# Fixed transfer order and GpSimd-issued shuffles in the first batch of a spectral mixture-of-experts kernel

## The chip, the cores and the metric

The kernel runs on one core of a Trainium2 chip. The metric is the device time of one execution in microseconds (us), lower is better. The engines are called by the profile's names: PE (TensorE matmul), PEld (its weight loads), DVE (VectorE), ACT (ScalarE), POOL (GpSimd) and SP (SyncE, which only issues transfers). ACT, POOL and SP each have a queue from which they can issue DMA transfers; the lines of the profile call these issues SPq, ACTq and POOL.

## The reference

```python
def _attn_ref(x, filt_r, filt_i):            # x [8, 3072, 256] float32
    X = np.fft.rfft(x, axis=1)
    return np.fft.irfft(X * (filt_r + 1j * filt_i)[None], n=3072, axis=1)

def _moe_ref(x, w_a, w_b, w_out):            # float64 weights, hidden size 1536
    return (x @ w_a) * (x @ w_b) @ w_out

def _moe2_ref(x, w_gate, w_output_gate, w1, w2):   # 8 experts, hidden size 1024
    logits = x @ w_gate
    e_idx = argmax(logits); p = softmax(logits)
    eom = sigmoid(x @ w_output_gate)
    out[mask_e] = p[mask_e, e] * eom[mask_e, e] * (relu(x[mask_e] @ w1[e]) @ w2[e])   # each expert e
```

The 24,576 tokens pass a spectral filter along the sequence, a gated feed-forward block, and then one of eight experts each.

## The kernel before, in words

The transform of length 3072 is split as 96 times 32. Stage 1 multiplies along the first factor, a shuffle of rows follows, stage 2 multiplies along the second factor, applies the filter and goes back over it, and stage 3 goes back over the first factor. After that the tokens go in 64 tiles of 384 through the first feed-forward block (`moe1`), whose 12 chunks of the hidden size (index f) each need a chunk of weights that has been turned from float64 into two float32 halves. Batches 1 to 7 are transformed beside the tiles of earlier batches. Batch 0 has nothing to run beside, and `conv_first` does it: this is the stage that the change touches, and the first tile of `moe1` waits for its end.

`conv_first` works as follows.

- Stage 1 has 16 steps u. Each loads a 192 KB tile of x (`load_x`, L310) on SP, multiplies it by f1f (L338) and copies the result on ACT (L339) into `stay`, a buffer on chip that later holds weight chunks 4 to 11. The x tiles rotate through 6 buffers, five of them filled ahead.
- Stage 2 has 12 units m. A unit reads its shuffled rows a2 (`load_a2`): two transfers of 128 KB from `stay` to an x-type buffer, each from 4 partitions to 128 partitions (L329). All 24 are issued from SP, four units ahead. All of stage 1 must be done before the first, since each reads all columns.
- A unit also needs `load_c`: the filter rows fg (256 KB, L315) and the matrices cr (384 KB, L322), on SP, three units ahead; unit 0 also reads fr (256 KB, L319).
- Then follow 4 matmuls into psx (L351), two shuffles of the filter on DVE (L364), two products px and qx on DVE (L367, L368), 8 matmuls into psb (L376), a copy on ACT (L379) and a 256 KB store to b_dr on ACT's queue (L380).
- After the last unit `s3_load` reads bt from b_dr on SP (L392), stage 3 runs on PE (L399), and the first tile of `moe1` begins (its first matmul is the one into pa at L113).

Beside it runs `weight_steps`. A chunk is loaded by three transfers of 256 KB on SP (L663 twice, L667) into one of four buffers. Step `first` works on ACT and DVE (L680 to L682), `second` on DVE, ACT and POOL (L687 to L694; the POOL product is L694), `third` on PE, ACT, POOL and DVE (L700 to L713; the POOL subtraction is L118, wab<-ws), `fourth` forms the gate columns (L720, L721). The load of chunk f + 4 has to wait for `second` of chunk f, whose buffer it takes. The loop in the program part says how many of these steps stand among the 40 steps of `conv_first`, from step n_first on; with N_EARLY = 3 there are 18 of them. The rest stand in the first tile of `moe1`, four per chunk.

The order in which each engine's queue takes its instructions is not the program's order: a scheduler in the build simulates the kernel and orders each queue by its own times. Only from tile 60 on is SP's order that of the program (`manual_schedule`).

Of the kernel before, what the change touches and what calls it, by code (L numbers as in the profile page):

```python
# [9 lines left out]
F32 = mybir.dt.float32  # L10
# [9 lines left out]
B, S, D = 8, 3072, 256  # L20
NTOK = B * S
NE, DFF, DFF2 = 8, 1536, 1024
# sequence index n = 32 * n1 + n2, frequency k = k1 + 96 * k2
N1, N2 = 96, 32
# [7 lines left out]
# routed tokens: expert e owns rows [e * CAP, (e + 1) * CAP) of the bucket buffer  # L32
# [3 lines left out]
def _phases():  # L36
    """Token counts per weight load, largest first, and how many such groups are sure to exist;
    the last kind has as many as could be needed."""
    out, used = [], 0
    for t, seen in ((2048, SNAP * MT), (1024, SNAP * MT), (512, NTOK)):  # L40
        n = -(-(seen - used - NE * (t - 1)) // t)
        out.append((t, n))
        used += t * n
    t = 256
    out.append((t, (NTOK - used + NE * (t - 1)) // t))
    return out
# [4 lines left out]
CAP = NTOK + T_B  # L51
DUMMY = NE * CAP
BIG_ID = 1 << 20
# high words, read as float32, of the float64 numbers 2**-126 and just under 2**128
F64_MIN, F64_MAX = (float(v) for v in np.array([897 << 20, (1151 << 20) - 1], np.int32).view(np.float32))
# batches that go through the convolution together, and the tiles in which they do
ROUNDS = (((1,), 1, 6), ((2, 3), 6, 16), ((4, 5), 16, 32), ((6, 7), 32, 48))
# chunks of the first block's weights that are ready before its first tile
N_EARLY = 3
# chunks whose place is not lent to the first convolution  # L60
F_STAY = FC - N2 * D // 1024
# groups of the last kind at its end that are run only if some token needs them
# [4 lines left out]
def spectral_moe_kernel(ctx: ExitStack, tc: tile.TileContext, a: dict, out: bass.AP):  # L67
# [30 lines left out]
    # by chunk of the hidden size: high and low halves of w_a and w_b  # L98
# [10 lines left out]
    def split3(ps, terms, start, stop):  # L109
        """Products of operands given as (high, low) pairs, all but low * low."""  # L110
        n = len(terms)
        for i, ((lh, ll), (rh, rl)) in enumerate(terms):
            nc.tensor.matmul(ps, lhsT=lh, rhs=rh, start=start and i == 0, stop=False)  # L113
            nc.tensor.matmul(ps, lhsT=lh, rhs=rl, start=False, stop=False)  # L114
            nc.tensor.matmul(ps, lhsT=ll, rhs=rh, start=False, stop=stop and i == n - 1)  # L115
# [5 lines left out]
    a_dr, b_dr = {}, {}  # L121

    def conv_steps(bs):
        """Emission steps of some batches' convolution, up to its inverse over n2; each step
        says whether it is of the tensor engine or of the others."""
        vp = pool["v"]
        nb = len(bs)
        # a unit of stage 2 is one group of rows of two batches, or two groups of one
# [77 lines left out]
        # stage 1  # L206
# [25 lines left out]
        # stage 2 and its inverse  # L232
# [61 lines left out]
    def conv_first():  # L294
        """The convolution of batch 0, before there is other work: the tensor engine has time
        for float32 products, which need no split operands, and for a product more instead of
        an exchange of rows. What stage 1 makes stays on chip, where weights come later."""
# [9 lines left out]
        def load_x(u):  # L307
            if u < half:
                xin[u] = vp.tile([N1, 2, D], F32, tag="xin", name="xin", bufs=6)
                nc.sync.dma_start(xin[u], xv[:, 2 * u : 2 * u + 2, :])  # L310

        def load_c(u):
            if u < n_u:
                fg[u] = mp.tile([128, 2, D], F32, tag=("xth", "xtl")[u % 2], name="fg")
                nc.sync.dma_start(fg[u], a["fri"][2 * u : 2 * u + 2].rearrange("t p d -> p t d"))  # L315
                if u == 0:
                    # its first row pairs two real frequencies: the real parts come row by row
                    fr0 = vp.tile([128, 2, D], F32, tag="fr", name="fr0")
                    nc.sync.dma_start(fr0, a["frfi"][0:2, :, 0].rearrange("t p d -> p t d"))  # L319
                    fg[0] = fg[0], fr0  # L320
                cr[u] = vp.tile([128, 3, 2, 128], F32, tag="cr", name="cr", bufs=6)
                nc.sync.dma_start(cr[u], a["c_first"][u])  # L322

        def load_a2(u):
            if u < n_u:
                a2[u] = vp.tile([128, 2, D], F32, tag="xin", name="a2", bufs=6)
                for j in range(2):
                    k = 4 * (2 * u + j)
                    nc.sync.dma_start(a2[u][:, j, :], stay[k : k + 4].rearrange("k (n d) -> k n d", d=D))  # L329

        for u in range(5):
            load_x(u)
        for u in range(half):
            load_x(u + 5)
            if u in (4, 6, 8):
                load_c(u // 2 - 2)
            p = ps_cv("ps1", 2 * D, N1)
            nc.tensor.matmul(p, lhsT=f1f, rhs=xin.pop(u).rearrange("p n d -> p (n d)"), start=True, stop=True)  # L338
            nc.scalar.copy(stay[:, 2 * D * u : 2 * D * (u + 1)], p)  # L339
            yield  # L340
        for u in range(4):
            load_a2(u)
        xx = {}
        for m in range(n_u + 1):
            load_c(m + 3)
            load_a2(m + 4)
# [87 lines left out]
    def gate_1(i):  # L434
        z = ztile[i]
        lg, og = z[:, :, D : D + NE], z[:, :, D + NE : D + 2 * NE]
        m = small("gm", [128, 3, 1])
        nc.vector.tensor_reduce(out=m, in_=lg, axis=AX.X, op=ALU.max)
        d = small("gd", [128, 3, NE])
        nc.vector.tensor_tensor(out=d, in0=lg, in1=bc(m), op=ALU.subtract)  # L440
        e = small("ge", [128, 3, NE])
        nc.scalar.activation(e, d, AF.Exp)
        # the first of equal maxima: the largest of 8 - index
        r = small("gr", [128, 3, NE])
        nc.vector.scalar_tensor_tensor(
            out=r, in0=d, scalar=0.0, in1=rev.unsqueeze(1).to_broadcast([128, 3, NE]), op0=ALU.is_ge, op1=ALU.mult
        )
        nc.vector.tensor_reduce(out=m, in_=r, axis=AX.X, op=ALU.max)
        oh = small("goh", [128, 3, NE])
        nc.vector.tensor_tensor(out=oh, in0=r, in1=bc(m), op=ALU.is_equal)  # L450
        ob = small("gob", [128, 3, NE], BF16)
        nc.vector.tensor_copy(ob, oh)
        osel = small("gos", [128, 3, NE])
        nc.vector.tensor_tensor(out=osel, in0=oh, in1=og, op=ALU.mult)
        o = small("go", [128, 3, 1])
        nc.vector.tensor_reduce(out=o, in_=osel, axis=AX.X, op=ALU.add)
        eo = small("geo", [128, 3, 1])
        nc.scalar.activation(eo, o, AF.Exp, scale=-1.0)
        gate[i] = (e, oh, ob, eo)
# [19 lines left out]
    def gate_2(i):  # L479
# [18 lines left out]
        # scale = 1 / (sum + 1e-9) / (1 + exp(-o))  # L498
# [63 lines left out]
    def plan(k, start, end):  # L562
        """Expert and first row of each group of kind k among the rows [start, end) of each
        expert; groups past the last one get the dummy rows. Returns the rows left."""
# [57 lines left out]
    def plan_rest(c):  # L622
# [3 lines left out]
        # rows past the last of each expert: no token, scale 0  # L626
# [7 lines left out]
    def load_consts():  # L634
        nc.sync.dma_start(sgn, a["c_sgn"])
        nc.sync.dma_start(f1f, a["c_f1f"])
        nc.sync.dma_start(w3, a["c_w3"])

    def load_consts_2():
        nc.gpsimd.dma_start(f1, a["c_f1"])  # L640
# [7 lines left out]
    def weight_steps():  # L648
        """Float64 weights, one 128-wide chunk of the hidden size at a time: float32 values from
        their bits, exact halves of these, and the gate columns."""  # L650
# [21 lines left out]
        def first(f):  # L672
# [6 lines left out]
            # magnitudes in float32's normal range; the exponent's offset 1023 becomes 127  # L679
# [16 lines left out]
        def third(f):  # L696
# [14 lines left out]
            # gate columns: w_out @ [w_gate | w_output_gate]  # L711
# [24 lines left out]
    # groups that share one load of weights, and their tiles of up to 512 tokens  # L736
# [98 lines left out]
    def l2(n, c):  # L835
# [6 lines left out]
        for j in range(nj):  # L842
            p = psy[n][j // 2][:, 256 * (j % 2) : 256 * (j % 2 + 1)]
            bl = slice(128 * j, 128 * (j + 1))
            # both halves of a bank accumulate; the first product issued there clears it
# [30 lines left out]
    def moe2_slot(n, c, pre=True):  # L876
        """Slot c of tile n of the routed block, with what its successors need."""
# [20 lines left out]

    load_consts()
# [9 lines left out]
    n_first = 8  # L909
    early = 4 * N_EARLY + 7  # L910
    done = 0
    for n, _ in enumerate(conv_first()):
        if n == 4:
            load_consts_2()
# [5 lines left out]
    s3_load(0)  # L920
    for k in range(2):
        s3_mm(0, k)
# [104 lines left out]
    # the last groups, which few distributions of the tokens need  # L1027
# [33 lines left out]
def _constants():  # L1061
# [46 lines left out]
    # of batch 0: also the matrix for the product with the filter's imaginary part, which  # L1108
    # enters the partner's row
# [52 lines left out]
```

## Time and profile before

| What | Value |
|---|---|
| Median of 3 runs | 4187.19 us (4184.61 to 4190.07) |
| Span of the profiled execution, first to last instruction | 4183.0 us |
| PE busy | 4064.7 us, 97% of the span |
| DVE, ACT, POOL busy | 2059.5 (49%), 1819.5 (43%), 724.5 us (17%) |
| DMA | 346.73 MB, mean 83 GB/s |

The profile gives the profiled execution by its span alone; the median of the timed runs is 4.2 us above that span, and that difference stands for what lies before the first and after the last instruction. A line of the timeline gives the start, the duration, the engine, the line of the kernel, the operation, out<-in and how many were merged (x4); in brackets stand the idle time of the engine ahead of it and what ended it. A line of the window view gives for each engine the busy time and the number of instructions, then the granted clock of TensorE (1.00 is 2.4 GHz, 0.50 is 1.2 GHz), the mean busy share of the 16 DMA engines and the bytes moved.

### The profile page before, as it was taken

What the parts mean: (1) busy time and instruction counts of PE and PEld (TensorE: products, weight loads), DVE (VectorE), ACT (ScalarE), POOL (GpSimd) and SP (SyncE); (2) the same over time, 40 slices, a digit from 0 to 9 for tenths busy, and PEclk for the clock granted to TensorE, in tenths of its full rate; (3) what the DMA queues carried; (4) which work ended last, traced back from release to release, by engine and by line L of the source; (5) the groups of instructions that cost most, each with busy time, mean ns of one, the idle gap of its engine ahead of it and who ended that gap; (6) DMA issues with size and microseconds to landing.
All of it is one profiled execution on the core that took longest, in us unless ns stands there. A gap on an engine that the chain in (4) does not pass through costs nothing. (4 is left out here: it accounts for less than half of the span.)

```text
span 4183.0 us, 68755 instructions
## 1 busy us (share of the span) xinstructions
PE 4064.7 (97%) x26500; PEld 3895.0 (93%) x26500; DVE 2059.5 (49%) x4496; ACT 1819.5 (43%) x3832; POOL 724.5 (17%) x672
## 2 busy tenths in 40 slices
PE   5699999999999999999999999999999999999998
PEld 2599999999999999999999999999999999999998
DVE  3556456644465554445554444445433333444575
ACT  2455455544444443444443333333333343444565
POOL 1313013310022210012221000000111111111211
PEclk7699999999999999999999999999999999999999
DMA  5444233312222211222221000001221222234364
GB/s 161 136 129 131 73 99 106 97 55 79 76 69 72 76 58 53 73 69 74 71 66 39 19 22 20 20 20 37 74 69 65 75 95 95 84 128 143 124 218 144
DMA packets 214625, 346.73 MB, mean 83 GB/s; under 512 B 22956, under 2 KB 134285, under 8 KB 214290
## 3 DMA queue, kind: packets, MB, share of 16 engines
q1 hardware_dynamic: 156658, 242.99, 19.2%
q10 hardware_dynamic: 38656, 47.20, 3.6%
q0 software_dynamic: 18976, 52.07, 3.4%
q8 instruction: 210, 3.44, 0.3%
q14 instruction: 125, 1.02, 0.1%
HBM read 237.50 MB, written 102.38 MB: 81 GB/s over the span
## 5 line engine op out<-in xcount | busy, mean ns | idle before, releaser
L540 ACT CAST gh<-g 128x384 fp32r<-128x384 f32 x768 | 394.1, 513 | 833.6 <-DVE g L539 818.8
L539 DVE TENSOR_TENSOR g<-asb,pb 128x384 f32<-128x384 f32 x768 | 424.3, 552 | 632.9 <-PE pb L115 617.1
L115 PE MATMUL po<-wo_h,gl 128*128 128x272 f32 x2304 | 664.6, 288 | 0.0
L114 PE MATMUL po<-wo_l,gh 128*128 128x272 f32 x2304 | 663.4, 288 | 0.0
L118 DVE TENSOR_TENSOR gl<-g,gh 128x384 fp32r<-128x384 f32 x768 | 464.3, 605 | 403.1 <-ACT gh L540 402.3
L113 PE MATMUL po<-wo_h,gh 128*128 128x272 f32 x2304 | 662.5, 288 | 0.0
L532 ACT COPY asb<-pa 128x384 f32<-128x384 f32 x768 | 368.6, 480 | 438.7 <-PE pa L115 437.1
L830 DVE SCALAR_TENSOR_TENSOR hl<-ph,hh 128x512 fp32r<-128x512 f32 (+1 forms) x464 | 284.1, 612 | 528.4 <-ACT hh L829 525.4
L113 PE MATMUL pa<-xth,wab 128*128 128x384 f32 x1536 | 537.2, 350 | 4.0 <-ACT asb L532 3.9
L113 PE MATMUL pb<-xth,wab 128*128 128x384 f32 x1536 | 518.0, 337 | 2.5 <-DVE g L539 2.4
L115 PE MATMUL pa<-xth,wab 128*128 128x384 f32 x1536 | 520.1, 339 | 0.0
L114 PE MATMUL pa<-xtl,wab 128*128 128x384 f32 x1536 | 518.9, 338 | 0.0
L114 PE MATMUL pb<-xtl,wab 128*128 128x384 f32 x1536 | 516.8, 336 | 0.0
L115 PE MATMUL pb<-xth,wab 128*128 128x384 f32 x1536 | 515.6, 336 | 0.0
L829 ACT ACTIVATE hh<-ph 128x512 fp32r<-128x512 f32 (+1 forms) x464 | 250.7, 540 | 547.0 <-PE ph L115 545.9
L503 POOL DMA_INDIRECT zbuf<-z,gpi x192 | 201.1, 1048 | 1636.6 <-ACT asb L532 1054.7
L113 PEld LDWEIGHTS po<-wo_h,gh 128*128 128x128 f32 x2304 | 434.3, 188 | 0.0
L115 PEld LDWEIGHTS po<-wo_h,gl 128*128 128x128 f32 x2304 | 433.3, 188 | 0.2 <-DVE gl L118 0.2
L114 PEld LDWEIGHTS po<-wo_l,gh 128*128 128x128 f32 x2304 | 432.7, 188 | 0.0
L864 POOL DMA_INDIRECT out<-y,z x198 | 204.4, 1032 | 954.2 <-ACT y L863 560.9
L113 PEld LDWEIGHTS pa<-xth,wab 128*128 128x128 f32 x1536 | 289.3, 188 | 16.5 <-ACT asb L532 5.2
L114 PEld LDWEIGHTS pa<-xtl,wab 128*128 128x128 f32 x1536 | 289.7, 189 | 9.5 <-DVE xtl L118 0.3
(178 smaller groups left out, 8078.2 us busy)
## 6 DMA issues: line engine op xcount, KB each, us to landing
raw<-in_moe_w SPq DMA_DIRECT2D x156, 512.0 KB
xin<-in_x SPq DMA_DIRECT2D x128, 192.0 KB
b_dr<-bsb ACTq DMA_DIRECT2D x96, 256.0 KB
bt<-b_dr SPq DMA_DIRECT2D x64, 384.0 KB
z<-zbuf SPq DMA_DIRECT2D x41, 544.0 KB
a_dr<-asb ACTq DMA_DIRECT2D x112, 192.0 KB
a<-a_dr SPq DMA_DIRECT2D x84, 256.0 KB
fg<-in_frfi SPq DMA_DIRECT2D x72, 256.0 KB
```

What stands on the lines that cost most here:

```text
L113: nc.tensor.matmul(ps, lhsT=lh, rhs=rh, start=start and i == 0, stop=False)
L114: nc.tensor.matmul(ps, lhsT=lh, rhs=rl, start=False, stop=False)
L115: nc.tensor.matmul(ps, lhsT=ll, rhs=rh, start=False, stop=stop and i == n - 1)
L118: eng.tensor_tensor(out=o, in0=x, in1=h.bitcast(F32), op=ALU.subtract)
L503: nc.gpsimd.indirect_dma_start(out=zbuf, out_offset=bass.IndirectOffsetOnAxis(ap=posi[:, j : j + 1], axis=0), in_=z[:, j, :], in_offset=No ...
L532: nc.scalar.copy(asb, pa)
L539: nc.vector.tensor_tensor(out=g, in0=asb, in1=pb, op=ALU.mult)
L540: nc.scalar.copy(gh, g)
L829: nc.scalar.activation(hh[:, :t], p[:, :t], AF.Relu)
L830: nc.vector.scalar_tensor_tensor(out=hl[:, :t], in0=p[:, :t], scalar=0.0, in1=hh[:, :t].bitcast(F32), op0=ALU.max, op1=ALU.subtract)
L864: nc.gpsimd.indirect_dma_start(out=out, out_offset=bass.IndirectOffsetOnAxis(ap=z[:, j, D + 1 : D + 2].bitcast(I32), axis=0), in_=y, in_of ...
```

## The change

The change concerns only what happens up to the end of batch 0's transform, with one constant for the weights. SP's transfers of that part keep the program's order (`manual_schedule` around it), and the program's order is rearranged: of the constants only f1f is loaded ahead of x, and x has 8 tiles ahead. The 24 shuffle transfers a2 are issued from GpSimd's queue instead of SP's, six units ahead. `load_c` of units 0 to 3 stands in stage 1 (at u = 3, 5, 7, 9), later ones behind a2 in their unit. N_EARLY goes from 3 to 4 and n_first from 8 to 6, so that 22 weight steps stand among the 40. Comments were taken out as well.

```diff
-N_EARLY = 3
+N_EARLY = 4
+AHEAD = 8
...
         def load_x(u):
             if u < half:
-                xin[u] = vp.tile([N1, 2, D], F32, tag="xin", name="xin", bufs=6)
+                xin[u] = vp.tile([N1, 2, D], F32, tag="xin", name="xin", bufs=AHEAD)
                 nc.sync.dma_start(xin[u], xv[:, 2 * u : 2 * u + 2, :])
...
         def load_a2(u):
             if u < n_u:
-                a2[u] = vp.tile([128, 2, D], F32, tag="xin", name="a2", bufs=6)
+                a2[u] = vp.tile([128, 2, D], F32, tag="xin", name="a2", bufs=AHEAD)
                 for j in range(2):
                     k = 4 * (2 * u + j)
-                    nc.sync.dma_start(a2[u][:, j, :], stay[k : k + 4].rearrange("k (n d) -> k n d", d=D))
-
-        for u in range(5):
+                    nc.gpsimd.dma_start(a2[u][:, j, :], stay[k : k + 4].rearrange("k (n d) -> k n d", d=D))
+
+        for u in range(AHEAD):
             load_x(u)
         for u in range(half):
-            load_x(u + 5)
-            if u in (4, 6, 8):
-                load_c(u // 2 - 2)
+            load_x(u + AHEAD)
+            if u in (3, 5, 7, 9):
+                load_c((u - 3) // 2)
...
-        for u in range(4):
+        for u in range(AHEAD - 2):
             load_a2(u)
         xx = {}
         for m in range(n_u + 1):
-            load_c(m + 3)
-            load_a2(m + 4)
+            load_a2(m + AHEAD - 2)
+            if m:
+                load_c(m + 3)
...
     def load_consts():
+        nc.sync.dma_start(f1f, a["c_f1f"])
+
+    def load_consts_2():
         nc.sync.dma_start(sgn, a["c_sgn"])
-        nc.sync.dma_start(f1f, a["c_f1f"])
         nc.sync.dma_start(w3, a["c_w3"])
-
-    def load_consts_2():
         nc.gpsimd.dma_start(f1, a["c_f1"])
...
+    stack_sp = ExitStack()
+    stack_sp.enter_context(tc.manual_schedule(engines={mybir.EngineType.SP}))
     load_consts()
...
-    n_first = 8
+    n_first = 6
     early = 4 * N_EARLY + 7
...
-        if n == 4:
+        if n == 5:
             load_consts_2()
...
     s3_load(0)
+    stack_sp.close()
```

## Rows read from the trace of the kernel before

**Rows 1.** The page: busy times of the engines, and PE in 40 slices.

```profile
PE 4064.7 (97%) x26500; PEld 3895.0 (93%) x26500; DVE 2059.5 (49%) x4496; ACT 1819.5 (43%) x3832; POOL 724.5 (17%) x672
PE   5699999999999999999999999999999999999998
```

**Rows 2.** Waits of PE, 0 to 168 us: us in total, times, longest.

```profile
PE psx L351 <- DMA cr<-in_c_first: 48.9, 9, 8.8
PE psx L351 <- DMA a<-stay: 14.9, 4, 7.8
```

**Rows 3.** Timeline of PE and ACT in the first batch.

```profile
30.33 0.58 ACT L339 COPY stay<-ps 96x512 f32<-96x512 f32 x1 [1.12 <-PE ps L338]
...
38.09 1.22 PE L351 MATMUL psx<-a,cr 128*128 128x256 f32 x2 [7.79 <-DMA a<-stay]
...
103.87 2.08 PE L351 MATMUL psx<-a,cr 128*128 128x256 f32 x4 [5.68 <-DMA cr<-in_c_first]
...
136.93 2.04 PE L351 MATMUL psx<-a,cr 128*128 128x256 f32 x4 [6.92 <-DMA cr<-in_c_first]
...
147.72 2.07 PE L351 MATMUL psx<-a,cr 128*128 128x256 f32 x4 [4.46 <-DMA cr<-in_c_first]
...
154.57 0.59 ACT L379 COPY bsb<-psb 128x512 f32<-128x512 f32 x1 [1.49 <-PE psb L376]
...
167.48 0.69 PE L113 MATMUL pa<-xth,wab 128*128 128x384 f32 x1
```

**Rows 4.** Timeline of SP's queue.

```profile
30.94 18.28 SPq L329 DMA_DIRECT2D a<-stay  x8
...
111.58 3.63 SPq L315 DMA_DIRECT2D fg<-in_fri  x1
115.32 3.41 SPq L322 DMA_DIRECT2D cr<-in_c_first  x1
118.78 3.88 SPq L329 DMA_DIRECT2D a<-stay  x2
...
141.45 0.39 SPq L315 DMA_DIRECT2D fg<-in_fri  x1
...
159.09 0.34 SPq L392 DMA_DIRECT2D bt<-b_dr  x1
```

**Rows 5.** Window view of chosen stretches.

```profile
20.00:30.00 10.00, 7.04 (x8) 1.86 (x8) 0.03 (x1) 1.75 (x3) 0.00 (x0) 0.64 1.04 280
35.00:40.00 5.00, 1.22 (x2) 0.50 (x2) 4.25 (x4) 3.82 (x6) 3.12 (x2) 0.50 0.22 27
45.00:50.00 5.00, 2.38 (x5) 1.52 (x6) 0.52 (x1) 0.00 (x0) 0.00 (x0) 0.50 0.25 69
100.00:140.00 40.00, 17.36 (x41) 12.30 (x42) 13.40 (x30) 5.24 (x8) 3.12 (x2) 0.56 0.45 112
```

**Rows 6.** DMA view, 35 to 50 us: packets, MB, share of 16 engines; issues.

```profile
q1 hardware_dynamic: 712, 0.71, 23.6%
...
a<-stay SPq DMA_DIRECT2D x6, 128.0 KB
```

**Rows 7.** Timeline of POOL: a transfer issued there, and a weight subtraction.

```profile
1.99 0.60 POOL L642 DMA_DIRECT2D trione<-in_c_trione  x1
...
42.61 1.26 POOL L118 TENSOR_TENSOR wab<-ws,wab 128x512 fp32r<-128x512 f32 x1 [0.73 <-ACT wab L707]
```

**Rows 8.** Groups by line, 0 to 168 us, POOL: busy, mean ns, idle before.

```profile
L694 POOL TENSOR_TENSOR ws<-wraw,ws 128x768 f32<-128x768 f32 x8 | 15.0, 1874 | 135.6 <-ACT wraw L693 133.6 <-DMA b_dr<-bsb 2.0
L118 POOL TENSOR_TENSOR wab<-ws,wab 128x512 fp32r<-128x512 f32 x8 | 10.9, 1366 | 4.4 <-ACT wab L707 3.6 <-DMA bt<-b_dr 0.7
```

**Rows 9.** Timeline of ACT in the first tile: chunks f = 1, 2 and 7.

```profile
174.37 0.48 ACT L532 COPY asb<-pa 128x384 f32<-128x384 f32 x1
...
177.11 0.49 ACT L532 COPY asb<-pa 128x384 f32<-128x384 f32 x1
...
200.78 0.48 ACT L532 COPY asb<-pa 128x384 f32<-128x384 f32 x1 [0.96 <-PE pa L115]
```

## The prediction

> **What bounds the kernel now.** I read the page first. PE is busy 97% of the span and shows nines in all slices but the first two and the last [rows 1]; so only time ahead of the point where PE becomes full can be saved, and the first slices (105 us each) hold the stage that is changed. Next the timeline: the first matmul of `moe1` starts at 167.48 us [rows 3]. That is the mark to watch. Up to it the stage has three pieces: stage 1 ends with the copy at 30.33, the twelve units run from the first psx at 38.09 to the last at 147.72, and the tail (last psb copy, store, bt, stage 3) takes 167.48 − 147.72 = 19.8 us. The units take 109.6 / 11 = 10.0 us each.
>
> Then the waits of PE: 48.9 us for cr, 14.9 us for a2 [rows 2]. So transfers are late, but which resource makes them so? SP's timeline shows it: in steady state fg, cr and the two a2 take 3.63, 3.41 and 3.88 us of SP, 10.9 us in all, just the unit of 11.0 us from 103.87 to 136.93, while an unhindered fg issue takes 0.39 [rows 3, 4]. SP is blocked inside its issues. Why, the stretch of 35 to 50 us tells, where a2 is all that is issued but for one fg: the DMA share is 0.22 to 0.25 and the rate 27 to 69 GB/s, against 1.04 and 280 GB/s at 20 to 30 us [rows 5, 6]. A share that stops at a quarter means that four of the 16 engines work: a transfer that reads 4 partitions is not spread further. Their backlog stops SP, and with SP everything else. Over 100 to 140 us the mean share is 0.45 [rows 5], so twelve engines idle more than half of the time.
>
> **Stage 1, x first.** Ahead of the last x tile the new order leaves f1f, the 16 x tiles (3.1 MB), loads of units 0 and 1 (1.6 MB) and small constants (0.3 MB): 5.0 MB, at 280 GB/s [rows 5] 18 us, from 2 us on: 20 us instead of 30.33. The first a2 was used 7.8 us after that [rows 3]; with the same distance the first psx comes at 28. POOL may have other work in front; the bounds for the first psx are 25 (a2 spread over engines lands faster) and 36 (some of the chunk work that ended at 43.9 [rows 7] precedes it), and I take 30. Two more buffers take nothing but memory; they allow the eight x in flight. They can also delay nothing, as an a2 six units ahead takes a buffer whose matmul was two units ago.
>
> **a2 leaves SP.** 24 issues go from SP's queue to POOL's. SP loses 3.88 us per unit directly and its stalls in fg and cr, if the ring that blocks is no longer full. The trace shows no shuffle issued from POOL. Its price on POOL: from below 0.60 us, a direct transfer there [rows 7]; from above 2.3 us, the mean of the same transfer as SP was stalled in it (18.28 / 8 [rows 4]); I take 0.60, as it is the only row of that queue. Per unit 1.2 us, and half a chunk's two POOL instructions, (1.87 + 1.37) / 2 = 1.6 us [rows 8]: 2.8 us of POOL, beside the DMA. At 2.3 us it is 6.2 us, still under the DMA term below.
>
> How the transfer then lies on the DMA engines is the open step. If it is spread, the unit's DMA work is what the share shows: 0.45 × 11.0 = 5.0 us on all 16, plus half a chunk of weights, 786 KB / 280 GB/s / 2 = 1.4 us: 6.4 us. PE's own work is less, 17.36 / 40 × 11.0 = 4.8 us at a granted clock of 0.56 [rows 5], near the 1.2 GHz level. I take 6.5 us per unit, with 5.0 (no more weights than in that window) and 8.2 (half way to the present pace, with imperfect overlap) as bounds.
>
> The row is the quarter share [rows 5, 6]. The Trainium skill, "DMA: Bandwidth & Descriptors", section "Why a DMA increments its semaphore by 16 and not by 1", says that the number of engines is the largest up to 16 that divides the slowest dimension of both sides, on SP always the lowest-numbered ones, on GpSimd's queue consecutive ones from a moving cursor. The trace agrees with four (0.25); the cursor is shown by no row here, and with it the sum is the one above. The same page, "Rules for kernel authors", speaks against the change: spreading transfers over issuing engines does not help bandwidth and saves issue time only. By that sentence alone the four busy engines would remain, which is the first rival.
>
> **Fixed order on SP.** Loads can no longer be moved past a waiting one. In the units SP would wait at a chunk load for its buffer (`second` of four chunks before) or at fg for the shuffle of the unit before; behind it are the next fg and cr, three units (19 us) ahead of their use, so waits of that size cost nothing. Bounds: 0, and 5 us in all once the lead is eaten; a gain from the order is already in stage 1. I take 0. At the end, loads of chunks 8 to 11 now follow bt, where before some went ahead; bt came at 159.09 [rows 4], and chunk 8 is used eight steps into the tile, over 20 us later. Nothing.
>
> **Weights.** 22 steps instead of 18 stand in the stage, but the shorter stage gives less idle time for more. Before, 8 of 12 chunks had their POOL product by 168 us [rows 8]; four were prepared inside the first tile, and its steps f = 2 to 7 took (200.78 − 177.11) / 5 = 4.73 us against 2.74 before [rows 9]: 10 us more, 2.5 per chunk. After, 5 chunks are sure (step 22 is `third` of chunk 4), 7 remain, three more: 7.5 us given back. Bounds: 0 (the scheduler prepares as many as before) and 14 (three whole steps of 4.73).
>
> **The sum.** Last psx at 30 + 11 × 6.5 = 101.5 instead of 147.7: 46.2 us less; the tail is unchanged; 7.5 given back: 38.7. From the span, 4183.0 − 38.7 = 4144.3; the median lies 4.2 above the span, so 4148.5 us. The fast ends together: first psx 25, pace 5.0, nothing given back: 80 instead of 147.7, 4119. The slow ends together: 36, 8.2 and 10 of the give-back: 126.2, less 21.5, plus 10: 4176.
>
> **Rivals.**
> *The quarter stays.* From POOL a2 still uses the same four engines. 0.71 MB in 15 us [rows 6] is 47 GB/s, so a unit's 262 KB take 5.5 us there; the rest of the unit's work is (5.0 × 16 − 4 × 5.5) / 16 = 3.6 us per engine, weights 1.4: 10.5 us, no better than the present 10.0. Only stage 1's 8 us are saved: 4179. For it: the access pattern is unchanged. Against it: another queue fills its rings in another way, and the blocked issues on SP go in any case.
>
> *POOL's order.* The scheduler puts the products of chunks 0 and 1 in front of the first a2, and they wait for their weights. These ended at 43.9 [rows 7]; the first psx then is near 44, 14 later than in my sum: 4162.5. For it: POOL waited 133.6 us for ACT at L694 [rows 8], so its in-order queue does stand still for weights. Against it: the present order has a2 right after stage 1, and in later units a2 is six ahead.
>
> *Slower: POOL's issue price.* If writing one a2's descriptors occupied POOL for long, the unit would be 2p + 1.6 us. It breaks even where 30 + 11 × pace = 147.7, pace 10.7, p = 4.55 us; at 5.5 us the pace is 12.6, the last psx at 168.6, 21 us later: 4208. For it: 128 pieces of 1 KB each, read and written on chip, were never issued there in this trace. Against it: 0.60 us for 128 pieces of 512 bytes [rows 7]. The Trainium skill, "SBUF — State Buffer", sections "SBUF: two separate sides" and the one behind it, warns of just such a stall: VectorE holds a port, GpSimd cannot write descriptors, and a transfer of 620 ns took about 3100. By that figure, an estimate, the pace is 7.8 us and the time 4163, inside the own range of my sum; no row here shows it.
>
> **How the numbers follow.** The sum's course 0.62, with its own range of 4119 to 4176; the quarter stays 0.14; POOL's order 0.12; slower by the issue price 0.06; 0.06 for what I don't see (a schedule that changes elsewhere). A difference under 0.2% (8.4 us) can't be told from no change. The quarter's 4179 lies on that edge, and I split it in halves. Faster: 0.62 + 0.12 + 0.07 + 0.02 = 0.83; same 0.07 + 0.03 = 0.10; slower 0.06 + 0.01 = 0.07. The range reaches from a little under the fast ends to the rival whose saving is stage 1 alone: 4112 to 4183.
>
> **What would show it.** Right: the first `moe1` matmul near 121 us, stage 1's last copy near 20, psx every 6 to 7 us, SP's fg and cr issues back at 0.4 to 0.5 us, DMA share over 0.7 through the units, POOL issues of some 0.6 us. The quarter's rival: psx every 10 us and a share near 0.45, with SP idle. POOL's order: psx not before 40, a2 behind L694. The issue price: a2 issues of several us on POOL, back to back. The give-back: steps of 4 to 5 us in the first tile for more chunks than before. The prediction is wrong if the mark at `moe1` moves by under 15 us, or if it moves by 45 and the end doesn't follow.

## The result, and the profile after

The changed kernel takes 4133.98 us (median of 4 runs, 4130.23 to 4137.86) against 4185.9 us for the kernel before on the same chip (4 runs): ratio 0.9881 [0.9867, 0.9895], 52 us less. The profiled span goes from 4183.0 to 4131.7 us, 51.3 less.

The page of the changed kernel, engine busy times, then PE and the DMA share in 40 slices:

```profile
PE 4050.2 (98%) x26500; PEld 3886.4 (94%) x26500; DVE 2056.8 (50%) x4496; ACT 1817.2 (44%) x3832; POOL 740.0 (18%) x696
...
PE   6899999999999999999999999999999999999998
...
DMA  9442333212222211222210000001222222234364
```

Beside [rows 1] PE's line differs in its first two slices alone, 6 and 8 instead of 5 and 6: PE fills earlier, and what was won lies ahead of that point. The last matmuls into psx (the first product of a unit) end the units; the first one into pa is the mark. Timeline of PE and ACT up to the mark, against [rows 3]:

```profile
28.30 0.58 ACT L341 COPY stay<-ps 96x512 f32<-96x512 f32 x1 [1.13 <-PE ps L340]
...
37.92 2.08 PE L354 MATMUL psx<-a,cr 128*128 128x256 f32 x4 [9.66 <-DMA a<-stay]
...
98.41 0.60 PE L354 MATMUL psx<-a,cr 128*128 128x256 f32 x2
...
105.71 0.57 ACT L382 COPY bsb<-psb 128x512 f32<-128x512 f32 x1
...
119.10 3.73 PE L402 MATMUL ps<-w,bt 96*128 96x96 f32 x16 [13.49 <-DMA bt<-b_dr]
122.61 0.69 PE L115 MATMUL pa<-xth,wab 128*128 128x384 f32 x1
```

The mark, `moe1`'s first matmul, comes at 122.61 instead of 167.48 (−44.9). Stage 1 ends only 2 us earlier, the first psx stands where it stood, the twelve units run at (98.41 − 37.92) / 11 = 5.5 us instead of 10.0, and the tail, from the last psx to the mark, has become longer: 24.2 instead of 19.8. The waits of PE up to the mark (us in total, times, longest), against [rows 2]:

```profile
PE ps L402 <- DMA bt<-b_dr: 13.5, 1, 13.5
PE psx L354 <- DMA a<-stay: 11.4, 3, 9.7
PE ps L340 <- DMA xin<-in_x: 8.3, 3, 3.9
PE psx L354 <- DMA cr<-in_c_first: 8.2, 2, 6.5
```

The 48.9 us for cr are 8.2 now; the longest wait is the one for bt. The windows (busy us and instructions of PE, PEld, DVE, ACT, POOL; then granted clock, DMA share, GB/s) and the DMA view of 30 to 50 us, against [rows 5, 6]:

```profile
30.00:50.00 20.00, 10.38 (x26) 6.92 (x27) 8.13 (x15) 5.07 (x6) 11.30 (x14) 0.54 1.09 231
60.00:80.00 20.00, 11.29 (x41) 8.42 (x40) 15.45 (x29) 8.32 (x16) 12.98 (x13) 0.83 0.95 192
105.00:119.00 14.00, 0.61 (x3) 0.19 (x1) 11.53 (x13) 8.08 (x13) 11.07 (x5) 0.67 0.57 154
```

```profile
q1 hardware_dynamic: 2457, 3.05, 57.6%
q0 software_dynamic: 1633, 1.57, 51.7%
...
a<-stay POOLq DMA_DIRECT2D x13, 128.0 KB, 11.6
```

The share is full where it was 0.22 to 0.25. SP's queue (q1) moves 3.05 MB in 20 us beside GpSimd's (q0), and a2, which is what q0 carries here, moves 1.57 MB / 20 us = 79 GB/s although one a2 takes 11.6 us to land at the median: many are in flight together. SP's queue in the new order (start, duration):

```profile
20.75 0.29 SPq L649 DMA_DIRECT2D iot<-in_c_iot  x1
21.88 0.80 SPq L312 DMA_DIRECT2D xin<-in_x  x2
...
85.59 0.39 SPq L317 DMA_DIRECT2D fg<-in_fri  x1
87.13 0.34 SPq L324 DMA_DIRECT2D cr<-in_c_first  x1
...
111.33 0.37 SPq L666 DMA_DIRECT2D wraw<-in_moe_w_a  x1
112.90 0.33 SPq L395 DMA_DIRECT2D bt<-b_dr  x1
```

POOL's issues of a2 (ns min/median/max), and the chunk product that SP's load at 111.33 waited for:

```profile
L331 POOL DMA_DIRECT2D a<-stay x24: 677/680/1092, 29.2 to 70.6; - x24
```

```profile
107.20 4.11 POOL L697 TENSOR_TENSOR ws<-wraw,ws 128x768 f32<-128x768 f32 x1 [6.08 <-ACT wraw L696]
```

### The profile page after: what moved, and what is told of

The parts are those of the page before. It is cut to its first block, busy times and chain, and to the rows that moved or that the text cites. A ratio compares the mean times of both kernels' runs of the same rounds, so it can differ in the third digit from the quotient of the medians.

```text
span 4131.7 us, 68769 instructions
## 1 busy us (share of the span) xinstructions
PE 4050.2 (98%) x26500; PEld 3886.4 (94%) x26500; DVE 2056.8 (50%) x4496; ACT 1817.2 (44%) x3832; POOL 740.0 (18%) x696
```

## The experiments

The mark is the start of `moe1`'s first matmul; "tile" is the time from it to the first asb copy of the second tile (the 13th asb copy); "chunks" counts the POOL products ws<-wraw ahead of the mark. All ratios are against the kernel before, run on the same chip. Last psx, mark and tile come from one profiled execution each, and two kernels were profiled twice: the changed one (e9) had its last psx 3.7 us later and its mark 0.3 us earlier, e8's kernel (e10) both 5 us later. Differences of that size between two marks settle nothing.

| Run | last psx | mark | tile | chunks | median us | ratio |
|---|---|---|---|---|---|---|
| before | 147.72 | 167.48 | 53.8 | 8 | 4185.9 | |
| changed | 98.41 | 122.61 | 49.4 | 9 | 4133.98 | 0.9881 [0.9867, 0.9895] |
| e1_order_only | 131.90 | 151.57 | 51.5 | 9 | 4165.93 | 0.9961 [0.9947, 0.9975] |
| e2_a2_pool_only | 98.47 | 122.95 | 53.1 | 8 | 4134.41 | 0.9884 [0.9867, 0.99] |
| e3_a2_act | 123.85 | 151.91 | 49.7 | 9 | 4160.18 | 0.995 [0.9933, 0.9967] |
| e4_a2_single_rows | 139.53 | 159.75 | 53.6 | 8 | 4175.13 | 0.998 [0.997, 0.999] |
| e5_all_rows_sp | 98.50 | 117.89 | – | 8 | 4150.03 | 0.9918 [0.9902, 0.9935] |
| e6_single_rows_pool | 116.19 | 137.81 | 53.3 | 8 | 4148.04 | 0.9914 [0.9897, 0.993] |
| e7_weights_late | 105.13 | 131.59 | 49.5 | 9 | 4141.65 | 0.9898 [0.9881, 0.9914] |
| e8_bt_first | 97.90 | 115.74 | 53.0 | 8 | 4129.42 | 0.9874 [0.9858, 0.9891] |
| e9_changed_again | 102.12 | 122.33 | 49.2 | 9 | 4134.07 | 0.9877 [0.986, 0.9893] |
| e10_bt_first_again | 102.95 | 120.73 | 54.6 | 8 | 4131.54 | 0.9871 [0.9855, 0.9887] |
| e11_shuffle_over_hbm | 83.68 | 105.23 | 52.8 | 8 | 4123.45 | 0.9857 [0.9841, 0.9874] |
| e12_hbm_shuffle_sp | 85.42 | 102.61 | 52.7 | 8 | 4118.38 | 0.9841 [0.9824, 0.9857] |

### Which part of the change: e1, e2, e3

e1 is the changed kernel with a2 back on SP:

```diff
-                    nc.gpsimd.dma_start(a2[u][:, j, :], stay[k : k + 4]...
+                    nc.sync.dma_start(a2[u][:, j, :], stay[k : k + 4]...
```

> The changed kernel with the 24 shuffle transfers a2 back on SP's queue; fixed order, 8 buffers and 4 early chunks stay. Theory (a2 is held to four of the 16 DMA engines on SP's queue, and their backlog stops SP): units stay at 9 to 11 us, the share of DMA near 0.45, first moe1 matmul at 155 to 175 us, 4175 to 4195 us. Rival (the fixed order and the buffers bring the gain, a2's queue doesn't matter): units of 6 us, first moe1 matmul near 125, 4130 to 4145 us.

e2 is the other half alone: the kernel before with `nc.gpsimd` for `nc.sync` in that line, six buffers, three chunks and the scheduler's order as they were.

> The kernel before with one edit: a2 is issued from GpSimd's queue. Theory (a2 spread over the engines is the gain): units of 6 to 7 us with a DMA share near 0.9, first moe1 matmul near 125 to 135, 4135 to 4150 us. Rival (order and buffers bring it): under 10 us of gain, 4175 to 4186 us.

e3 is the changed kernel with `nc.scalar` in that line.

> The changed kernel with a2 issued from ACT's queue instead of GpSimd's: SP is free of a2 as in the changed kernel. Theory (four engines are the limit, whoever of SP and ACT issues): the share of DMA falls back to about half, units of 9 to 11 us, ACT stopped in its a2 issues for 1 to 4 us each, 4170 to 4195 us. Rival (it is enough that SP is rid of a2): units of 6 to 7 us, 4130 to 4145 us.

The first matmuls of the timeline of e2, first unit and mark:

```profile
40.97 4.17 PE L351 MATMUL psx<-a,cr 128*128 128x256 f32 x8 [9.50 <-DMA a<-stay]
...
122.95 0.69 PE L113 MATMUL pa<-xth,wab 128*128 128x384 f32 x1
```

a2's queue alone gives the whole gain: e2's mark is 0.3 us from the changed kernel's and its median 0.4, both a little under the theory's ranges. The order alone (e1) was expected to bring next to nothing (4175 to 4195 us) and missed that: it is worth 17 us, at a pace of (131.90 − 41.90) / 11 = 8.2. Why its pace is better than 10.0 I have not separated; beside a2 on GpSimd it adds nothing to the mark. On ACT's queue the issues block just as they did on SP (ns min/median/max):

```profile
L331 ACTq DMA_DIRECT2D a<-stay x24: 544/1511/4163, 29.1 to 107.3; - x24
```

ACT, which also copies and stores, is thereby stopped for up to 4.2 us an issue. Its window of 30 to 50 us:

```profile
30.00:50.00 20.00, 7.22 (x14) 4.36 (x15) 3.67 (x7) 3.57 (x4) 0.00 (x0) 0.50 0.51 144
```

The DMA share is 0.51 where the changed kernel's is 1.09, as the theory had it; the time was missed by both (4160.18 us). To free SP is thus not enough; e3 lies near e1 and not near e2.

### Four engines, or four rows: e4, e5, e6

e4 takes the kernel before and splits each a2 on SP into four transfers of 32 KB that read one partition each, for the same bytes; e6 is the same on GpSimd's queue.

```diff
-                    nc.sync.dma_start(a2[u][:, j, :], stay[k : k + 4]...
+                    for q in range(4):
+                        nc.sync.dma_start(a2[u][32 * q : 32 * q + 32, j, :], stay[k + q : k + q + 1]...
```

> The kernel before with each a2 transfer on SP split into four, one source partition of 32 KB to 32 partitions each: 96 issues instead of 24, same bytes and pieces of 1 KB. Theory (the number of engines is the limit, and a transfer of 32 rows can be laid on 16 engines): the stretch in which only a2 runs shows a share near 1 instead of 0.25, units of 7 to 8 us, 4150 to 4165 us. Rival (reading one or four partitions is the limit, 27 GB/s as at 35 to 40 us of the kernel before, however many engines read): a high share but no higher rate, 262 KB at 27 GB/s or 9.7 us per unit during which all engines are held: 4185 to 4230 us.

Window and DMA view of e4, where little else runs:

```profile
36.00:50.00 14.00, 9.76 (x30) 7.24 (x30) 11.18 (x18) 6.01 (x11) 9.00 (x6) 0.53 0.77 41
```

```profile
q1 hardware_dynamic: 836, 0.57, 76.8%
...
a<-stay SPq DMA_DIRECT2D x18, 32.0 KB, 4.3
```

The share rises from a quarter to 0.77, and the rate stays: 41 GB/s against 47 before (0.71 MB in 15 us, [rows 6]). Per busy engine that is 41 / (0.77 × 16) = 3.3 GB/s against 47 / (0.236 × 16) = 12.4. More engines moved nothing more. But the edit changes two things: each transfer is laid on more engines, and it reads one partition instead of four (and writes 32 instead of 128). So such a narrow transfer can hold the engines, whatever their number; that this was the limit before, with four partitions, does not follow. Both expected times were missed (mark −7.7, median 8 us less). Two stretches of the kernel before in which a2 alone is under way say more:

```profile
33.00:41.00 8.00, 1.22 (x2) 0.50 (x2) 7.15 (x8) 5.60 (x8) 4.09 (x3) 0.50 0.22 26
45.00:49.00 4.00, 1.38 (x3) 0.70 (x4) 0.52 (x1) 0.00 (x0) 0.00 (x0) 0.50 0.24 70
```

Per busy engine that is 26 / (0.22 × 16) = 7.4 GB/s at first and 70 / (0.24 × 16) = 18 later, at the same quarter share and with the same kind of transfer.

e5 leaves a2 on SP and changes the source: each half unit is read from the last column block of all 96 partitions, and of 32 of them again, in two transfers. It leaves out the shuffle's contents.

```diff
-                    nc.sync.dma_start(a2[u][:, j, :], stay[k : k + 4]...
+                    nc.sync.dma_start(a2[u][:N1, j, :], stay[:, (N2 - 1) * D :])
+                    nc.sync.dma_start(a2[u][N1:, j, :], stay[: 128 - N1, (N2 - 1) * D :])
```

> The kernel before, a2 on SP, but a2 reads the last column block of all 96 rows of stay (and 32 rows a second time, in a transfer of its own) instead of 4 rows: same bytes and pieces of 1 KB, 48 issues; the shuffle's contents are left out, so the tokens of batch 0 are other values. Theory (what makes a2 slow on SP is that one transfer at a time is read, from 4 partitions, at 41 to 47 GB/s): with the source spread over partitions the stretch of a2 alone runs at over 150 GB/s, units of 6 us, first moe1 matmul at 115 to 130, 4125 to 4145 us, with SP issuing. Rival (a2 has to leave SP's in-order queue, whatever it reads): units stay near 9 to 10 us, 4165 to 4185 us.

The first of its two lines of issues (ns), a window with a2 alone, and its mark:

```profile
L328 SPq DMA_DIRECT2D a<-stay x24: 522/540/891, 33.0 to 88.2; - x24
```

```profile
36.00:43.00 7.00, 3.15 (x8) 2.06 (x8) 6.22 (x6) 4.69 (x7) 3.97 (x3) 0.50 0.37 99
```

```profile
117.89 0.69 PE L113 MATMUL pa<-xth,wab 128*128 128x384 f32 x1 [0.22 <-ACT xth L415]
```

On SP's own queue these issues take 0.54 us at the median and at most 0.89, and the mark is 5 us ahead of the changed kernel's, no more than two executions differ by. The theory's mark came true; its rate (over 150 GB/s) and its time did not. Its end can't be compared: with other values the tokens go to other experts, and PE runs 26,600 matmuls instead of 26,500. The share of 0.37 shows that e5 also has more than a quarter of the engines at work, so it does not separate source and engines either. Per busy engine it moves 99 / (0.37 × 16) = 17 GB/s. That is what the kernel before had at 45 to 49 us too: there its engines were not slower than with a wide source, they were few. At 33 to 41 us they were slower as well.

> The kernel before, a2 on GpSimd's queue, each transfer split into four of one source partition and 32 KB (96 issues). Theory (on GpSimd's queue it is several transfers side by side, on different engines and different source partitions, that bring the rate; a single-row transfer takes all engines and they read one partition at a time): a2 falls back to 40 to 50 GB/s, units of 9 to 11 us, 4165 to 4190 us. Rival (GpSimd's queue is fast for another reason, such as its own ring or its packets of 4 KB): POOL's 8 issues of 0.68 us and 1.6 us of weights give units of 7 us, 4140 to 4150 us.

```profile
45.00:50.00 5.00, 3.80 (x13) 2.73 (x12) 3.67 (x8) 1.34 (x2) 4.62 (x10) 0.76 0.84 34
```

In this window of e6 there is a2 and next to nothing from SP: 34 GB/s at a share of 0.84. So single rows are slow on GpSimd's queue too, as the theory said, but by its time the rival held. An own queue took the mark from 159.75 (e4) to 137.81 (e6), −22 us, and four rows in one transfer from there to 122.95 (e2), −15. These 15 us have two possible causes that no run separates, the read of single rows and the number of issues:

```profile
L330 POOL DMA_DIRECT2D a<-stay x96: 496/496/766, 31.3 to 110.6; - x96
```

In a unit POOL issues for 8 × 0.50 = 4.0 us instead of 2 × 0.68 = 1.4, and the pace is (116.19 − 39.18) / 11 = 7.0, the figure that the rival had worked out from the issues.

### The start and the tail: e7, e8, e9, e10

e7 is the changed kernel with the constants and the weight steps later, to let x and the first a2 through:

```diff
-    n_first = 6
+    n_first = 14
...
-        if n == 5:
+        if n == 9:
             load_consts_2()
```

> The changed kernel with the constants behind all x loads (n == 9) and the weight steps starting after the first units' a2 (n_first = 14): about 3 MB less ahead of x and of the first a2. Theory (from 20 us on the DMA engines are full, so the bytes up to the last unit decide, and what is moved back has to come later): the first psx comes 8 to 12 us earlier, at 26 to 30, but the first moe1 matmul moves by under 5 us; 4128 to 4137 us. Rival (the late start of stage 2 sets the end): the first moe1 matmul at 112 to 115, 4122 to 4127 us.

```profile
L312 SPq DMA_DIRECT2D xin<-in_x x16: 312/422/586, 1.2 to 15.1; - x16
27.43 0.58 ACT L341 COPY stay<-ps 96x512 f32<-96x512 f32 x1 [1.13 <-PE ps L340]
36.11 1.22 PE L354 MATMUL psx<-a,cr 128*128 128x256 f32 x2 [8.71 <-DMA a<-stay]
```

Both missed: the first psx moves by 1.8 us, no more than in the changed kernel's second profile (36.66 in e9), the pace is 6.3, and the mark is 9 us later. The last x is issued at 15.1 instead of 22.3, and stage 1 ends at 27.43, against 28.30 in the changed kernel and 27.51 in e9. So it is not the early weights and constants alone that hold stage 1 and the first psx. That the weight work pushed back is what costs the 9 us is likely and not shown.

e8 takes SP's fixed order off before the last loads of chunks, so that bt can go first; e10 is the same kernel again, beside the changed kernel again (e9).

```diff
-    stack_sp.close()
...
+            stack_sp.close()
```

> The changed kernel with SP's fixed order kept through the first tile, so that bt is issued ahead of the loads of chunks 8 and 9, which in the changed kernel went in front of it and waited for POOL. Theory (bt stood 2 to 3 us behind that wait and 3 us behind those bytes): first moe1 matmul 4 to 6 us earlier, at 117 to 119; the chunks then come later, 0 to 4 us lost in the first tile: 4128 to 4134 us. Rival (the first tile waits for its weights, so an earlier start is given back in full or more): 4134 to 4142 us.

```profile
106.46 0.32 SPq L395 DMA_DIRECT2D bt<-b_dr  x1
```

> The changed kernel itself, to set the two kernels of this group against it on one chip. Both theories: 4130 to 4138 us, a ratio to the kernel before of 0.987 to 0.989.

> The kernel with SP's order fixed through the first tile (bt ahead of two chunk loads) once more, with more rounds. Theory (its first tile starts 7 us earlier and gives about half of it back): 3 to 6 us under the changed kernel. Rival (the difference of 4.6 us was chance): within 1.5 us of the changed kernel.

The last psx and the mark of e10, then the last psx of e9:

```profile
102.95 0.59 PE L354 MATMUL psx<-a,cr 128*128 128x256 f32 x2
120.73 0.69 PE L115 MATMUL pa<-xth,wab 128*128 128x384 f32 x1 [1.56 <-ACT xth L418]
```

```profile
102.12 0.60 PE L354 MATMUL psx<-a,cr 128*128 128x256 f32 x2
```

e8's tail is 115.74 − 97.90 = 17.8 and e10's the same, instead of 24.2 in the changed kernel and 20.2 in e9. But the ninth chunk, whose load now stands behind bt, is no longer prepared in the stage, and the tile takes 53.0 and 54.6 instead of 49.4 and 49.2: half or more of it is given back. At the end 4.6 us are left in the first pair, which was not run side by side (2.9 us by the two ratios), and 2.5 in the second; the intervals overlap in both: not settled, and in any case small.

### Without the narrow read: e11, e12

Stage 1's result is stored to HBM as it is made (16 stores of 192 KB from ACT), and a2 is read back from there, one transfer of 256 KB a unit. That doubles the shuffle's bytes. bt goes first as in e8. e11 reads on GpSimd's queue, e12 on SP's.

```diff
+        s_dr = dp.tile([N1, N2, D], F32, tag="s_dr", name="s_dr", bufs=1)
+        sv = s_dr.rearrange("k n d -> (k n) d").rearrange("(t p) d -> p t d", p=128)
...
-                for j in range(2):
-                    k = 4 * (2 * u + j)
-                    nc.gpsimd.dma_start(a2[u][:, j, :], stay[k : k + 4]...
+                nc.gpsimd.dma_start(a2[u], sv[:, 2 * u : 2 * u + 2, :])
...
+            nc.scalar.dma_start(s_dr[:, 2 * u : 2 * u + 2, :], stay[:, 2 * D * u : 2 * D * (u + 1)]...
```

> As the kernel with bt first, but each pair of stage 1's columns is stored to HBM from ACT's queue when it is copied (16 stores of 192 KB), and a2 is read back from there, one transfer of 256 KB from HBM to 128 partitions per unit on GpSimd's queue; the values are the same. Theory (reading 4 partitions at a time is what holds the DMA engines, 0.52 of all 16 at 30 to 50 us of the changed kernel): 3.1 MB more are moved, but in pieces that take 50 to 110 ns; units of 4.5 to 5.5 us, first moe1 matmul at 105 to 112, 4118 to 4126 us. Rival (the engines are full of bytes, so 3.1 MB more at 280 GB/s cost 11 us): first moe1 matmul at 120 to 130, 4130 to 4142 us.

> As the kernel with the shuffle over HBM, with a2's 12 transfers issued from SP instead of GpSimd. Theory (it is the reading of 4 partitions that made SP's queue stand still, so once that is gone the queue doesn't matter): first moe1 matmul at 103 to 112, 4119 to 4128 us, SP's issues at 0.3 to 0.6 us. Rival (transfers have to leave SP's in-order queue in any case): first moe1 matmul at 118 or later, 4132 us or more.

Windows of e12 and its a2 issues (ns):

```profile
30.00:50.00 20.00, 5.72 (x15) 2.94 (x14) 8.70 (x10) 11.27 (x16) 6.56 (x4) 0.50 0.97 303
50.00:80.00 30.00, 26.30 (x118) 21.38 (x117) 28.61 (x63) 12.18 (x22) 6.25 (x4) 0.97 0.95 316
```

```profile
L331 SPq DMA_DIRECT2D a<-s_dr x12: 359/360/425, 40.8 to 70.1; - x12
```

The mark comes at 105.23 (e11) and 102.61 (e12), 17 and 20 us ahead of the changed kernel's, and 10 to 18 ahead of those with bt first (e8, e10). The DMA share is about what it was there, 0.95 to 0.97 against 0.95 to 1.09, but it now carries 303 to 316 GB/s instead of 192 to 231; from 50 to 80 us PE is busy for 26.3 of 30 us. With the narrow read gone SP's queue serves as well as GpSimd's: 4118.38 us against 4123.45. e12 beats both kernels, the changed one by 16 us; their two ratios' intervals don't touch. Of e10, which has bt first as well, it is 13 us ahead.

## Why the prediction was right, and where it was not

**a2 leaves SP: right, and it is the whole gain.** Forecast were a mark at 121.3 and a span of 4144.3; measured 122.6 and 4131.7. SP's last issues of fg and cr are back at 0.3 to 0.4 us, though as long as a2 was under way some still took up to 4.37, and 40 of the 49 us that PE waited for cr are gone. The issue price on POOL was to be 0.60; it is 0.68 at the median and 1.09 at most, so the slower rival falls. A stall like the one that the Trainium skill warns of ("SBUF — State Buffer", cited there) was not seen: eight of the issues fall into the window of 60 to 80 us, where VectorE was busy for 15.45 of 20 us, and none of the 24 came near 3 us. Whether VectorE ran there in the mode that the warning is about, the views don't show. The quarter's rival falls by the share of 0.95 to 1.09, and POOL's order by a first psx at 37.92 that waited for a2 itself.

**The mark is right by errors that cancel, which is luck.** Stage 1 was to end at 20 and ended at 28.30. SP's fixed order put x 14 and 15 (issued at 21.88) behind the constants, but that is not the cause by itself: in e7 the last x is issued at 15.1, and stage 1 ends at 27.43. What holds it stays open. First psx was 30, with bounds 25 to 36, and is 37.92, outside: x first gained nothing, +8. The pace was 6.5 and is 5.5: −11 over eleven units. The tail was to stay at 19.8 and is 24.2: +4.4, as PE's wait for bt grew from 9.2 to 13.5 us. In e9, the same kernel, the three were +6.7, −6.0 (pace 5.95) and +0.4.

**Fixed order, "Nothing" at the end: wrong by 2 to 4 us.** I looked at loads that follow bt. The harm was in one ahead of it: the load at 111.33 waits for chunk work on POOL that ends at 107.20 + 4.11 = 111.31, and bt stands behind it and leaves at 112.90, 7.2 us after the last bsb copy (105.71). e8 and e10 show it by moving bt, which leaves there 3.1 us after that copy (106.46 after 103.36, 111.45 after 108.36). So the wait cost 4.1 us here, and 2.1 in e9 (112.48 after 107.27). It is not the fixed order's own: in e2, without it, the scheduler also puts such a load (111.53) ahead of bt (113.11), and the tail is 24.5.

**The give-back: the mis-sized term.** Of the miss of 12.6 us (4144.3 to 4131.7) it is 11.9: I forecast +7.5, and the tile took 49.4 instead of 53.8 us, −4.4. (The mark was 1.3 late, and 2.0 came later in the span.) I reasoned that a shorter stage prepares fewer chunks: 5 sure, three short. That set two different counts against each other: 5 counted chunks up to `third` in the program's steps, 8 counted POOL products in the schedule. By the program's steps the POOL product (`second`) of 5 chunks lies within the 18 steps before and of 6 within the 22 after; the schedule had 8 and 9 ahead of the mark, three more each time. The table refutes the reasoning too: in every run there were at least 8, even where the mark was at 102.61. Where it was 8 the tile took 52.7 to 54.6 us, where it was 9 it took 49.2 to 51.5. So the term has two values, near 0 and −2 to −5; one chunk is worth that much of the tile. Nine came in every run with N_EARLY = 4 in which bt was not put first, eight in all others, so N_EARLY alone is not the count. My lower bound, 0 for "as many as before", left out that it could be one more. What the ninth chunk is worth at the end is not settled: e2, with 8, has the same mark and a tile 3.7 us longer, but only 2.4 us of that are left in the profiled spans (4134.1 and 4131.7) and 0.4 in the medians. That the tile gives nothing back is shown by both.

**The mechanism: the quarter share holds, and it is not the whole.** The prediction read the quarter share as four engines at work and counted on GpSimd's queue to spread a2. There, at 30 to 50 us, a2 keeps 0.517 × 16 = 8.3 engines busy instead of 3.8 and moves 79 instead of 47 GB/s; on ACT's queue (e3), with SP free of a2, the share falls back to 0.51. On SP and on ACT the slow read also blocked all behind it. What the prediction left out is that a narrow source slows the engines themselves: 3.3 and 34 / (0.84 × 16) = 2.5 GB/s per busy engine with single rows (e4, e6), 79 / 8.3 = 9.5 in the changed kernel, 17 in e5. The full share of the changed kernel is therefore partly engines that wait: 0.95 carried 192 GB/s, and 316 in e12. How the gain divides between SP set free, more engines and several reads side by side stays open: e4 and e6 change the number of engines and the source together, and so do e5 and e12. The 15 us between e6 and e2 are no measure of it, because of the issues on POOL. That transfers in flight read different rows at once is a likely reason for the 79 GB/s; the views here don't show it piece by piece.

The Trainium skill, "DMA: Bandwidth & Descriptors", section "Rules for kernel authors", says that spreading transfers over issuing engines gives no bandwidth and saves issue time only. It did not hold for this transfer: with one queue changed a2's rate rose from 47 to 79 GB/s, and e2 gained 49 us. By e12 against e11 it did once the read was wide: there SP's queue was no worse than GpSimd's.

## What to carry to other kernels

Read the DMA share and the rate together where one transfer runs alone: divide the rate by the busy engines and set it against a transfer with a wide source. Few busy engines at a full rate each are one fault, many at a low rate each another, and an experiment that changes both at once doesn't tell which it was. A transfer like this one, which reads few partitions and blocks its queue, should not stand in a queue that others need, and a detour over HBM with twice the bytes can be cheaper than it. When a stall goes, look for the next in-order wait ahead of the stage's last load, and count the prepared work instead of taking it from the length of the stage.

## What was not expected of the hardware

- On-chip transfers of 128 KB from 4 partitions ran at 27 to 69 GB/s on SP's queue ([rows 5]), and those of 32 KB from one partition at 41 (SP) and 34 GB/s (GpSimd), with three to four times as many engines busy. In the same queue and at the same quarter share the rate per busy engine went from 7.4 to 18 GB/s within 16 us. The same bytes read back from HBM stood in windows of 303 to 338 GB/s.
- An issue from ACT's queue blocks like one from SP's: 1.5 us at the median and up to 4.2 for a2, beside 0.31 us for e12's 192 KB stores from the same queue.
- GpSimd's queue took the same transfers at 0.68 us each (1.09 at most), while one took 11.6 us to land at the median.
